# Four value tiles of the softmax branch computed in query rounds 7 to 10 and moved into their place by DMA

## The chip, the cores and the metric

The kernel runs on one core of one Trainium2 chip. The metric is device time in microseconds (us) of one launch; the time before is the median of three runs, 1008.59 us (1005.69 to 1008.81). The profile is one separate execution of the same kernel. PE is TensorE, DVE is VectorE, ACT is ScalarE, POOL is GpSimd, and SP is the engine that issues the DMAs.

## What is computed

Two attention branches over the same x (2048 tokens, 448 features, 16 heads of 28) are mixed by a gate for each token:

```python
x = A_x
g = sigmoid((x * gate_w).sum(-1, keepdims=True))
a = linear_attention(x, A_wqkv, w_phi) @ A_wo      # phi = [softmax(p), softmax(-p)], o = phi_q (phi_k^T v) / (phi_q sum phi_k)
b = softmax_attention(x, B_wqkv) @ B_wo            # softmax(q k^T / sqrt(28)) v
return g * a + (1 - g) * b
```

All is float32; products with x use a high part and a low part of each operand, so that one 128-token tile of a projection is 11 matmuls of 128x448.

## The kernel before, in words

**Front.** x, its parts and the queries and keys of branch B are made first (a scratch array in DRAM, `qkd`, holds the latter). Then one loop (L763) walks over rounds i = 0 to 42. In rounds 0 to 15 it makes the keys' features and the values of branch A and sums them (L483). From i = 16 on the round has a second number, q = i - 16, and this text counts by q, 0 to 26.

**The query rounds.** In rounds q = 0 to 15 PE multiplies x tile q with the folded query weights (`pq`, L801), ACT copies it out (`pcq`, L449), DVE and POOL make the two-sided softmax features of it (L451 to L469, with the exponential on ACT, L460). Three rounds later PE transposes the features (`pft`, L533), and ACT copies them to `fT` (L536). Every second round multiplies the features of 256 tokens with the summed keys and values: `numer(k)`, `pn`, L547, for blocks k = 0 to 7 in round 2k + 5. What follows for a block is a chain over several engines:

- `normalize1` (round 2k + 5): ACT copies the numerators out (`oUa`, L407), and two DMAs gather the denominators (`dena`, L410).
- `normalize2` (end of round 2k + 6): DVE takes the reciprocal (L416, L417), two DMAs write it to DRAM (`rda`, L421), and one DMA reads it back spread over the partitions (`rsa`, L422, 512 KB).
- `normalize3` (round 2k + 9): DVE multiplies (L428).
- `normalize4` (round 2k + 10): ACT rounds it (`oTa`, L436), POOL makes the low part (L437), both in two halves.
- `out_a` (rounds 2k + 11 and 2k + 12): PE multiplies with the output weights (`poa`, 12 matmuls at L117; the third of them is the first to read the low part of the first half), ACT scales by the gate into one of two buffers (`ga`, L599), and a DMA stores that (`gad`, L600).

From round 11 on each round also has one `mx_unit` (`pmb`, `pmd`, L293): scores of branch B whose row maxima are needed later; ACT and DVE reduce them (L296, L298).

**The value tiles of branch B.** In rounds 18 to 25, at the end of the round, `value_b(0)` to `value_b(7)` (L747) make the values of x tiles 0 to 7: 11 matmuls into `pvb`, and one ACT copy into `vb[0]` (L750), the first of two tiles of 8 x 16 x 32 a partition. `vb[0]` is opened in round 18 (L850 to L852), when the features' pool is closed, because it lies in that pool's memory; POOL then sets its columns 28 to 31 (L743, L744). Column 28 is 1.0, so that the product with the values gives the denominator too. After the loop, the value tiles 8 to 15 follow with the last mx units between them (L984 on), and then the softmax attention (L1191 on), whose first read of `vb[0]` is at L1069.

**What sets the order.** The orders of PE, DVE, ACT and POOL are those of the program text: a waiting instruction holds up all behind it on its engine. SP's order is made by a scheduler. All DMAs go through SP's one queue, and the listing of SP's order shows that the DMAs take eight semaphores in turn: a DMA whose semaphore was used eight DMAs before waits until that one has landed, unless it is known already.

PSUM tiles of the front come from four banks in rotation (`ps_s`, L48).

Of the kernel before, what the change touches and what calls it, by code (L numbers as in the profile page):

```python
# [8 lines left out]
F32 = mybir.dt.float32  # L9
# [8 lines left out]
P = 128  # L18
S = 2048
D = 448  # L20
H = 16
DH = 28
GW = 112
NG = 4
NT = S // P
# [15 lines left out]
def gated_mix_kernel(ctx, tc, xT, wqkB, wvB, wvA, wkAT, wqAT, phi, woA, woB,  # L41
# [7 lines left out]
    nc = tc.nc  # L49
# [14 lines left out]
    def ps_s(nm):  # L64
        if turn4:
            turn4.append(nm)
            if len(turn4) % 4 == 0:
                return ps_pv(nm)
        return ps.tile([P, 512], F32, tag="s", name=nm, bufs=psn[0])
# [38 lines left out]
    def weights(place, nm):  # L108
        if place == 1:
            return wp.tile([P, 2, 4, 512], F32R, tag="w1", name=nm)  # L110
        if place == 2:
            return front.tile([P, 2, 4, D], F32R, tag="w2", name=nm)
        return wp.tile([P, 2, 4, 450], F32R, tag="w3", name=nm)
# [13 lines left out]
    def tok_major(dst, t, w, n, mid=None):  # L127

        todo = [(x, w[:, i, b, :n]) for b, x, i in x3(slice(t * P, (t + 1) * P))]
        if mid is None:  # L130
            run(dst[:, :n], todo)
            return
        for i, (l, r) in enumerate(todo):
            mid(i)
            nc.tensor.matmul(dst[:, :n], l, r, start=i == 0, stop=i == len(todo) - 1,  # L135
                             skip_group_check=True)
# [36 lines left out]
    def take_acts():  # L173
        while acts:
            acts.pop(0)()
# [91 lines left out]
    def mx_unit():  # L267

        u = mxs["u"]
        if u == NF:  # L270
            return
        mx_fin()
        take_diffs(2)
        mxs["u"] = u + 1
        gq, r = divmod(u, 16)
        g, qb = divmod(gq, NQ)
        if gq < GM:
            c, qt = divmod(r, 4)
            hp, b = divmod(c, 2)
            col = 64 * gq + 16 * b + 4 * qt + 2 * hp  # L280
            if r in (4, 9):
                pair_query(gq + 1, r // 9)
        else:
            c, qt = divmod(r, QM)
            hp, b = divmod(c, 2)
            col = 64 * gq + 4 * QM * b + 4 * qt + 2 * hp
            if r == 0:
                mx_query(gq)
        qc, kc = mxs[("qp", gq, hp)], mxs[("kp", g, c)]
        pb, pd = ps_mx(f"pmb{u}", False), ps_mx(f"pmd{u}", True)  # L290
        for j in range(4):
            js = slice(32 * j, 32 * j + DH)
            nc.tensor.matmul((pb if j < 2 else pd)[:, j % 2, :], qc[js, qt * P:(qt + 1) * P],  # L293
                             kc[js, :], start=True, stop=True, tile_position=(32 * j, 0))
        rl = rlp.tile([P, 2, 512], F32, tag="rl", name=f"rl{u}", bufs=2 if psn[1] == 3 else 1)
        nc.scalar.activation(rl, pd, AF.Relu)  # L296
        for i in range(2):
            nc.vector.tensor_tensor_reduce(rl[:, i, :], pb[:, i, :], rl[:, i, :], 1.0, LOWEST,  # L298
                                           ALU.add, ALU.max, part[:, col + i:col + i + 1])
        if gq < GM and qt == 3 and qb == NQ - 1:  # L300
            pair_load(g + 1, c)
        if gq == GM and qt == QM - 1:
            mx_load(g, c)
        if r == 15:
            mx_reduce(gq)
# [157 lines left out]
    def features2(f, nm):  # L463

        f2 = f[:, :, :2 * DH].rearrange("p h (s f) -> p h s f", f=DH)
        sm = bd.tile([P, H, 2], F32, tag="fsum", name=f"fsum{nm}", bufs=3)
        nc.vector.tensor_reduce(sm, f2, AX.X, ALU.add)
        nc.vector.reciprocal(sm, sm)
        nc.gpsimd.tensor_mul(f2, f2, sm.unsqueeze(3).to_broadcast([P, H, 2, DH]))  # L469
        return f.rearrange("p h f -> p (h f)")  # L470
# [3 lines left out]
    def take_exps(left=0):  # L474
        while len(exps) > left:
            exps.pop(0)()
# [29 lines left out]
    def kv_copy():  # L506

        kvT = ta.tile([P, 2, 512], F32, tag="rs", name="kvT", bufs=2)[:, 0, :]
        k4 = kvT.rearrange("p (g i f) -> p g i f", i=2, f=64)
        nc.gpsimd.memset(k4[:, :, :, 56:], 0.0)  # L510
        nc.scalar.copy(
            k4[:, :, :, :56],
            pkv[:, :224].rearrange("p (g f) -> p g f", f=56).unsqueeze(2).to_broadcast([P, NG, 2, 56]))
        return kvT
# [72 lines left out]
    def load_split(w, nm):  # L587
        for i in range(2):
            nc.sync.dma_start(f32(w[:, i, :, :D]), w_d[nm][:, i])
# [157 lines left out]
    def value_b(t, mid=None):  # L747
        pv = ps_s(f"pvb{t}")
        tok_major(pv, t, wvB_s, D, mid)
        nc.scalar.copy(vb[t // 8][:, t % 8, :, 0:DH], pv[:, :D].rearrange("p (h d) -> p h d", d=DH))  # L750

    pace = {}

# [9 lines left out]
    for i in range(2 * NT + 11):  # L763
        t, q = i, i - NT
        y = q - 1
        tb = y // 2
        take_acts()
        if t < NT and t % 2 == 0:
            mx_unit()
            passes = (55 if t < NT - 4 else 44) + (4 if t >= 4 else 0)  # L770
            pace["n"] = 4 if t >= 4 else 0
            pace["at"] = [passes // 3, 2 * passes // 3] if t in (4, 6, 8) else [passes // 2]
        if q in (0, 1):
            take_exps()
        if part_low:
            part_low.pop()()
        if q == 0:
            woA_s = weights(3, "woA_s")
            wvB_s = weights(2, "wvB_s")
            load_split(woA_s, "woA")  # L780
            load_split(wvB_s, "wvB")

        if t % 2 == 0 and 0 <= t - 4 < NT:
            kv_add(t - 4)
            kv_add(t - 3)
        if q == 2:
            bk_s.close()
            ta_s = ExitStack()
            ta = ta_s.enter_context(tc.tile_pool(name="ta", bufs=1, reuse_waits="tile"))
            KV = ta.tile([P, 512], F32, name="KV")  # L790
            kvT = kv_copy()
            turn4.append("")
            take_exps()
        if t < NT:
            pk = ps_s(f"pk{t}")
            tok_major(pk, t, wkA_s, D, tick)
            fk[t] = features1(pk, f"k{t}", nc.gpsimd)
            take_exps(1)
        if 0 <= q < NT:
            pq = ps_s(f"pq{q}")  # L800
            tok_major(pq, q, wqA_s, D)  # L801
        if q == 0:
            fk[NT - 1] = features2(fk[NT - 1], f"k{NT - 1}")
        if q in (1, 2):
            fq[q - 1] = features2(fq[q - 1], f"q{q - 1}")
        if 0 <= q < NT:
            fq[q] = features1(pq, f"q{q}", nc.vector if 0 < q < 11 else nc.gpsimd)
        if 0 <= t - 1 < NT - 1:
            fk[t - 1] = features2(fk[t - 1], f"k{t - 1}")
        if q in (0, 1) or q >= 11:  # L810
            mx_unit()
        if y >= 9 and y % 2 and tb - 4 < 8:
            oTs[tb - 4] = normalize4(ta, num.pop(tb - 4), f"a{tb - 4}", 2)
        if y >= 4 and y % 2 == 0 and tb - 2 < 8:
            numer(tb - 2)
        if q > 0:
            take_exps(int(q < NT))
        if q == 3:
            kv_out(kvT)
        if 2 <= q - 1 < NT:  # L820
            fq[q - 1] = features2(fq[q - 1], f"q{q - 1}")
        take_subs()
        if t == 1:
            pair_load(0, 3)
        if y >= 8 and y % 2 == 0 and tb - 4 < 8:
            num[tb - 4] = normalize3(*num[tb - 4], 2)
        if t < NT:
            value_a(t)
            if t % 2 and t < NT - 4:
                proj_qk(NP + t // 2, ev)  # L830
                if t < 8:
                    part_low.append(part_high(t // 2))
        if q in (0, 1):
            proj_qk(NP + 6 + q, ev)
        take_lows()
        if 2 <= i < 6:
            fold(wqA_s, "q", i - 2)
        if q == 1:
            ev_s.close()
        if q == 1:  # L840
            gates()
        if y < 9 or y % 2:
            if y >= 2 and y - 2 < NT:
                turn(y - 2)
        if 0 <= y - 10 < NT:
            out_a(y - 10)
            out_a2(y - 10)
        if y >= 9 and y % 2 == 0 and y - 2 < NT:
            turn(y - 2)
        if q == NT + 2:  # L850
            bd_s.close()
            vb = [value_tile(0)]  # L852
        if 0 <= q - NT - 2 < 8:
            value_b(q - NT - 2)
        if y >= 5 and y % 2 and tb - 2 < 8:
            num[tb - 2] = normalize2(ta, *num[tb - 2], f"a{tb - 2}", 2, True)
    ta_s.close()
# [442 lines left out]
```

## Time and profile before

| | |
|---|---|
| median of 3 runs | 1008.59 us |
| the profiled execution's own time | 1007.98 us |
| its span (first to last instruction) | 1006.2 us |
| PE busy | 997.0 us (99% of the span) |
| ACT, DVE, POOL busy | 80%, 67%, 24% |
| mean granted TensorE clock | 0.998 |
| rounds q = 7 to 10 | 200.2 to 215.0 us |
| rounds q = 18 to 26 | 262.9 to 310.7 us |

How to read a row of a timeline: start in us, duration in us, engine, line and operation, output<-inputs, sizes, how many instructions were merged, and in square brackets the idle time of that engine before the row with what ended it. A row of a table by windows has, for each engine, busy us and in brackets the number of instructions, in the order PE, weight load, DVE, ACT, POOL, and at its end the granted TensorE clock, the busy share of the 16 DMA engines and GB/s.

### The profile page before, as it was taken

The numbers are of one execution on the slowest core, as the hardware profiler recorded it, in microseconds if no ns is written. First come the engines' busy times: TensorE is split into PE (matmuls) and PEld (weight loads), VectorE is DVE, ScalarE is ACT, GpSimd is POOL, SyncE is SP. The second block draws the span as 40 slices with busy tenths as digits, with TensorE's granted clock in tenths as the row PEclk, the third lists the DMA queues.
The fourth block names the chain that finished last, engine by engine and source line by source line (L and its number), as shares of the span: only waits on it lengthen the run. The fifth ranks groups of instructions, "written<-read, shape, count | busy, mean of one in ns | idle before, by whom it ended". The sixth has DMA issues, their size and how long they took to land.

```text
span 1006.2 us, 17986 instructions
## 1 busy us (share of the span) xinstructions
PE 997.0 (99%) x6472; PEld 556.3 (55%) x6472; DVE 679.2 (67%) x1340; ACT 803.4 (80%) x1532; POOL 237.4 (24%) x215
## 2 busy tenths in 40 slices
PE   9999999989999999999999999999999999999998
PEld 8878888868888433333333333333333334455656
DVE  5557766997535688888888888888887874544202
ACT  5445545667743899999999999999999999979682
POOL 1265456687436103111011110101201011001010
PEclk9999999999999999999999999999999999999999
DMA  8976313312235703333532123431324345515131
GB/s 296 313 234 212 118 50 108 113 47 82 92 116 137 158 10 84 83 75 77 120 69 75 44 67 86 102 90 49 90 52 97 81 98 145 147 38 148 60 107 55
DMA packets 67769, 106.23 MB, mean 106 GB/s; under 512 B 18368, under 2 KB 28208, under 8 KB 67680
## 3 DMA queue, kind: packets, MB, share of 16 engines
q1 hardware_dynamic: 67680, 105.08, 38.6%
q8 instruction: 51, 0.84, 0.4%
q14 instruction: 38, 0.31, 0.1%
HBM read 73.21 MB, written 31.45 MB: 104 GB/s over the span
## 4 chain that ended last, share of the span: by engine, by line
PE 77%; DVE 0%; ACT 0%; issue 0%
PE st L965 28%; PE pv L1069 25%; PE pm L330 9%; PE poa L117 4%; PE pob L117 3%; PE pvb L135 2%; PE pvb L117 2%; PE pq L117 1%; PE pmb L293 1%; PE pft L533 1%; PE poL L1107 1%; PE pn L547 1%; PE poL L1177 0%; DVE part L341 0%; PE pr L1162 0%; PE pd L1152 0%
## 5 line engine op out<-in xcount | busy, mean ns | idle before, releaser
L968 ACT ACTIVATE p<-st 128x512 f32<-128x512 f32 x1020 | 529.3, 639 | 25.7 <-PE st L965 25.7
L341 DVE TENSOR_REDUCE part<-pm 128x1 f32<-128x512 f32 x477 | 304.7, 685 | 134.8 <-PE pm L330 134.8
L965 PE MATMUL st<-qst,kst 128*128 128x512 f32 x1020 | 303.1, 423 | 0.4 <-DVE acc L1084 0.4
L1069 PE MATMUL pv<-p,vb 128*32 128x512 f32 x2048 | 266.1, 603 | 0.0
L965 PEld LDWEIGHTS st<-qst,kst 128*128 128x128 f32 x1020 | 167.9, 187 | 99.4 <-ACT p L968 48.9
L334 ACT ACTIVATE rl<-pm 128x512 f32<-128x512 f32 x212 | 132.2, 624 | 15.5 <-PE pm L330 13.4
L330 PEld LDWEIGHTS pm<-kc,qc 28*128 28x128 f32 x848 | 40.5, 181 | 177.8 <-issue 104.8
L428 POOL TENSOR_TENSOR oUb<-oUb,rsb 128x512 f32<-128x512 f32 x15 | 19.4, 1291 | 457.0 <-DMA rsb<-rdb 212.2
L338 DVE CUSTOM_DVE_ANT_0 rl<-pm,rl 128x512 f32<-128x512 f32 x159 | 108.2, 681 | 0.0
L330 PE MATMUL pm<-kc,qc 28*128 28x512 f32 x848 | 107.3, 495 | 0.0
L1069 PEld LDWEIGHTS pv<-p,vb 128*32 128x32 f32 x2048 | 45.4, 108 | 94.1 <-issue 87.4
L298 DVE CUSTOM_DVE_ANT_0 rl<-pmb,rl 128x512 f32<-128x512 f32 x88 | 56.6, 681 | 36.9 <-ACT rl L296 36.9
L117 PE MATMUL pqk<-XH,wB 128*128 128x512 f32 x192 | 59.3, 397 | 0.0
L296 ACT ACTIVATE rl<-pmd 128x1024 f32<-128x1024 f32 x44 | 45.4, 1031 | 8.2 <-PE pmd L293 4.5
L623 ACT CAST ev<-pqk 128x512 fp32r<-128x512 f32 x28 | 16.1, 589 | 38.6 <-PE pqk L117 28.8
L117 PE MATMUL poa<-woA_s,oTa 128*128 128x448 f32 x192 | 44.6, 382 | 0.0
L117 PEld LDWEIGHTS pqk<-XH,wB 128*128 128x128 f32 x192 | 35.4, 188 | 8.5 <-issue 1.5
L1084 DVE SCALAR_TENSOR_TENSOR acc<-pob,gate,acc 128x448 f32<-128x448 f32 x12 | 8.2, 681 | 47.2 <-PE pob L117 47.2
L117 PEld LDWEIGHTS poa<-woA_s,oTa 128*128 128x128 f32 x192 | 35.9, 194 | 6.9 <-issue 4.2
L204 POOL TENSOR_TENSOR kc<-kc,kd 28x512 fp32r<-28x512 f32 x12 | 15.4, 1281 | 101.6 <-DMA kc<-qkd 45.8
L624 DVE TENSOR_TENSOR ev<-pqk,ev 128x512 fp32r<-128x512 f32 x28 | 19.1, 690 | 28.8 <-ACT ev L623 28.7
L135 PE MATMUL pva<-wvA_s,XH 128*128 128x450 f32 x128 | 37.6, 371 | 0.0
(163 smaller groups left out, 1175.8 us busy)
## 6 DMA issues: line engine op xcount, KB each, us to landing
qkd<-ev SPq DMA_DIRECT2D x28, 512.0 KB
qst<-qkd SPq DMA_DIRECT2D x64, 224.0 KB
kst<-qkd SPq DMA_DIRECT2D x64, 224.0 KB
od<-oTb SPq DMA_DIRECT2D x48, 112.0 KB
rsa<-rda SPq DMA_DIRECT2D x8, 512.0 KB
rsb<-rdb SPq DMA_DIRECT2D x15, 256.0 KB
kc<-qkd SPq DMA_DIRECT2D x64, 56.0 KB
gad<-ga SPq DMA_DIRECT2D x16, 224.0 KB
```

Source lines behind the costliest of these rows:

```text
L117: nc.tensor.matmul(dst, l, r, start=i == 0, stop=i == len(todo) - 1)
L135: nc.tensor.matmul(dst[:, :n], l, r, start=i == 0, stop=i == len(todo) - 1, skip_group_check=True)
L296: nc.scalar.activation(rl, pd, AF.Relu)
L298: nc.vector.tensor_tensor_reduce(rl[:, i, :], pb[:, i, :], rl[:, i, :], 1.0, LOWEST, ALU.add, ALU.max, part[:, col + i:col + i + 1])
L330: nc.tensor.matmul(pm[j], mxs[("qc", gq)][js, qt * P:(qt + 1) * P], mxs[("kc", g, kb)][js, :], start=True, stop=True, tile_position=(32 * ...
L334: nc.scalar.activation(rl, pm[kb], AF.Relu if kb < 3 else AF.Copy)
L338: nc.vector.tensor_tensor_reduce(r, pm[j], r, 1.0, LOWEST, ALU.add, ALU.max, part[:, col + j:col + j + 1])
L341: nc.vector.tensor_reduce(part[:, col + j:col + j + 1], pm[j], AX.X, ALU.max)
L428: (nc.gpsimd if n == 1 else nc.vector).tensor_mul(oU, oU, rs)
L965: nc.tensor.matmul(st, kst_of[(gq // NQ, kt // 4)][:, j, (kt % 4) * P:(kt % 4 + 1) * P], qst_of[gq][:, j, :], start=True, stop=True)
L968: nc.scalar.activation(p, st, AF.Exp, scale=SCALE)
L1069: nc.tensor.matmul(pv[32 * j:32 * j + 32, :], vb[kt // 8][:, kt % 8, 4 * g + j, :], pt[j], start=kt == 0, stop=kt == NT - 1, tile_position ...
```

## The change

Four value tiles (0 to 3) are computed behind the query tiles of rounds 7 to 10. They go into two tiles of their own (`ve0`, `ve1`, 4 KB a partition each), made in round 2, whose columns 28 to 31 POOL sets then. When `vb[0]` is opened in round 18, two DMAs of 512 KB copy them into it. The value tiles 4 to 7 follow in rounds 18 to 21, so that rounds 22 to 25 have none. The number of matmuls and of ACT copies is unchanged; four POOL memsets and two DMAs are added.

```diff
     def value_b(t, mid=None):
         pv = ps_s(f"pvb{t}")
         tok_major(pv, t, wvB_s, D, mid)
-        nc.scalar.copy(vb[t // 8][:, t % 8, :, 0:DH], pv[:, :D].rearrange("p (h d) -> p h d", d=DH))
+        v = early[t // 2][:, t % 2] if t < 4 else vb[t // 8][:, t % 8]
+        nc.scalar.copy(v[:, :, 0:DH], pv[:, :D].rearrange("p (h d) -> p h d", d=DH))
...
             kvT = kv_copy()
+            early = [ta.tile([P, 2, 512], F32, tag="rl2", name=f"ve{i}", bufs=2) for i in range(2)]
+            early = [e.rearrange("p t (h d) -> p t h d", d=32) for e in early]
+            for e in early:
+                nc.gpsimd.memset(e[:, :, :, 28:], 0.0)
+                nc.gpsimd.memset(e[:, :, :, 28:29], 1.0)
...
             fk[t - 1] = features2(fk[t - 1], f"k{t - 1}")
+        if 7 <= q < 11:
+            value_b(q - 7)
         if q in (0, 1) or q >= 11:
             mx_unit()
...
         if q == NT + 2:
             bd_s.close()
             vb = [value_tile(0)]
-        if 0 <= q - NT - 2 < 8:
-            value_b(q - NT - 2)
+            for k, e in enumerate(early):
+                nc.sync.dma_start(vb[0][:, 2 * k:2 * k + 2], e)
+        if 0 <= q - NT - 2 < 4:
+            value_b(q - NT + 2)
```

## Prediction

> **What bounds the kernel now.** I read the page first: is there an engine that never rests?
>
> ```profile
> span 1006.2 us, 17986 instructions
> PE 997.0 (99%) x6472; PEld 556.3 (55%) x6472; DVE 679.2 (67%) x1340; ACT 803.4 (80%) x1532; POOL 237.4 (24%) x215
> ```
>
> PE is busy 99% of the span. Work that is moved on PE but not removed can gain only where PE stands still, or where its clock is low. So I next read PE's timeline over the query rounds, and then a table by windows around the one large gap.
>
> ```profile
> 217.38 0.50 PE L293 MATMUL pmd<-kp,qp 28*128 28x512 f32 x2
> 221.00 1.55 PE L547 MATMUL pn<-fT,KV 56*32 56x256 f32 x32 [3.12 <-ACT fT L536]
> 222.47 3.89 PE L117 MATMUL poa<-woA_s,oTa 128*128 128x448 f32 x12
> ...
> 217.80:221.00 3.20, 0.08 (x5) 0.01 (x1) 3.07 (x5) 2.52 (x5) 1.94 (x2) 1.00 0.24 93
> 221.00:226.50 5.50, 5.50 (x47) 3.99 (x48) 5.42 (x11) 3.82 (x7) 5.31 (x5) 0.69 0.15 45
> ...
> 266.00:311.00 45.00, 44.70 (x253) 36.42 (x251) 15.42 (x41) 22.09 (x36) 12.77 (x12) 1.00 0.34 106
> 311.00:330.00 19.00, 18.58 (x94) 15.92 (x95) 11.32 (x14) 6.80 (x11) 14.52 (x10) 1.00 0.83 173
> ```
>
> In round 11 PE stands still for 3.12 us until ACT has copied `fT`. Then the granted clock is 0.69 for 5.5 us, which loses 5.5 x 0.31 = 1.70 us. The gap is worth 3.12 + 1.70 = 4.82 us. From 266 to 330 us PE stands still for 0.30 + 0.42 us in all, so the rest of the front has nothing to gain. Why was `fT` late? The timelines of ACT, DVE and SP:
>
> ```profile
> 218.48 1.14 ACT L436 CAST oTa<-oUa 128x512 fp32r<-128x512 f32 x2 [3.58 <-DVE oUa L428]
> 219.53 0.94 ACT L460 ACTIVATE feat<-feat 128x896 f32<-128x896 f32 x1
> 220.38 1.05 ACT L536 COPY fT<-pft 128x512 f32<-128x512 f32 x2
> ...
> 215.75 2.70 DVE L428 TENSOR_TENSOR oUa<-oUa,rsa 128x1024 f32<-128x1024 f32 x1 [0.23 <-DMA rsa<-rda]
> ...
> 207.89 0.54 SPq L422 DMA_DIRECT2D rsa<-rda  x1
> ```
>
> ACT stood 3.58 us before the first `oTa` for DVE's product with block 0's `rsa`, and `fT` was behind it on ACT. That `rsa`, 512 KB, took 215.75 - 207.89 = 7.86 us to land. So the gap comes from block 0's normalisation chain, not from PE's own work.
>
> **The change part by part.** *Moved tiles.* One value tile and one `out_a` on the chain of waits, and the starts of `pq` in rounds 7, 10 and 11 on PE's timeline:
>
> ```profile
> 300.00 2.27 PE pvb L117 x11
> 308.06 2.65 PE poa L117 x12
> ...
> 200.20 0.65 PE L117 MATMUL pq<-wqA_s,XH 128*128 128x448 f32 x2
> 211.86 0.64 PE L117 MATMUL pq<-wqA_s,XH 128*128 128x448 f32 x2
> 214.96 0.65 PE L117 MATMUL pq<-wqA_s,XH 128*128 128x448 f32 x2
> ```
>
> A tile is 2.27 us of PE, so four are 9.08 us. They are added ahead of round 11 and taken out of rounds 22 to 25. Of the first part the gap should swallow 4.82. With three tiles before it, `pq` of round 10 starts at 211.86 + 6.81 = 218.7, three us after `rsa` has landed, and ACT does its casts, exponential and first `fT` copy (1.14 + 0.85 + 0.5) behind the fourth tile's copy at 218.7 + 2 x 2.27 + 0.5 = 223.7, by 226.2; PE arrives at `pn` only at 217.88 + 9.08 = 227.0. So round 18 starts 9.08 - 4.82 = 4.26 us later than before.
>
> The four ACT copies move with their tiles; ACT has room in rounds 7 to 10, where a round of PE grows from (214.96 - 200.20) / 4 = 3.7 to 6 us.
>
> *Memsets in round 2.* Four of POOL, like this one:
>
> ```profile
> 183.43 0.15 POOL L510 MEMSET kvT<- 128x64 f32 x1
> 186.83 1.71 POOL L469 TENSOR_TENSOR feat<-feat,fsumq 128x896 f32<-128x896 f32 x1 [3.25 <-ACT pcq L449]
> 267.76 0.53 POOL L743 MEMSET vb<- 128x512 f32 x1
> ```
>
> Between 0.15 and 0.53 us each, 0.6 to 2.1 together, in a POOL gap of 3.25 us. I cost them at nothing; without that cover they would cost at most 2.1.
>
> *What the tail gives back.* If PE never waited in rounds 18 to 26, they would end 9.08 earlier relative to their start, and the sum would be -4.82. But blocks 6 and 7 have the same chain, and I now read SP and DVE there. All times that follow are on the scale of before, as if round 18 began at the same moment.
>
> ```profile
> 264.69 0.54 SPq L422 DMA_DIRECT2D rsa<-rda  x1
> 267.02 1.24 SPq L421 DMA_DIRECT2D rda<-dena  x2
> 275.15 0.55 SPq L422 DMA_DIRECT2D rsa<-rda  x1
> 275.80 1.18 SPq L410 DMA_DIRECT2D dena<-oUa  x2
> 284.91 1.14 SPq L421 DMA_DIRECT2D rda<-dena  x2
> 287.87 0.55 SPq L422 DMA_DIRECT2D rsa<-rda  x1
> ...
> 273.61 1.23 DVE L428 TENSOR_TENSOR oUa<-oUa,rsa 128x1024 f32<-128x1024 f32 x1 [1.58 <-DMA rsa<-rda]
> 284.31 0.18 DVE L416 TENSOR_SCALAR dena<-dena 128x32 f32<-128x32 f32 x1 [5.91 <-DMA dena<-oUa]
> 297.58 1.23 DVE L428 TENSOR_TENSOR oUa<-oUa,rsa 128x1024 f32<-128x1024 f32 x1 [3.13 <-DMA rsa<-rda]
> ```
>
> Three `rsa` (blocks 5, 6, 7) follow one another. Block 5's takes 273.61 - 264.69 = 8.92 us, block 7's 297.58 - 287.87 = 9.71. A tiny `dena` issued right behind block 6's lands 8.5 us later, while `rda` with nothing ahead needs 287.87 - 285.48 = 2.39 from its second issue (284.91 + 0.57), 1.8 of it after the issue: small DMAs stand behind an `rsa`. This chain runs at the DMAs' pace, not at PE's. How near is PE to it already?
>
> ```profile
> 298.02 0.64 ACT L599 ACTIVATE ga<-poa,gate 128x448 f32<-128x448 f32 x1 [4.91 <-DMA gad<-ga]
> 298.55 0.52 ACT L750 COPY vb<-pvb 128x448 f32<-128x448 f32 x1
> 298.97 1.04 ACT L296 ACTIVATE rl<-pmd 128x1024 f32<-128x1024 f32 x1
> 299.88 1.15 ACT L436 CAST oTa<-oUa 128x512 fp32r<-128x512 f32 x2
> ...
> 300.59 2.53 POOL L437 TENSOR_TENSOR oTa<-oUa,oTa 128x512 fp32r<-128x512 f32 x2 [8.46 <-ACT oTa L436]
> ...
> 302.63 2.73 PE L117 MATMUL poa<-woA_s,oTa 128*128 128x448 f32 x12
> ```
>
> POOL has the first low half at 300.59 + 1.27 = 301.86; the third matmul of `out_a(14)` at 302.63 + 0.44 = 303.07 needs it. The slack is 1.2 us. Between `numer(7)` and `out_a(14)` stood six value tiles and now stand three: PE arrives 6.81 us earlier, and finds nothing.
>
> *The moves* sit in that chain. In the listing of the changed order SP issues the first `rda` of block 6, a move, a `gad`, the other move, and then the second `rda`. The first move waits for POOL's memsets of `vb[0]` (the first of the two ends at 268.3), and the second `rda` takes the semaphore of block 5's `rsa`, so it leaves only at 273.6; behind it wait block 7's `dena` and block 6's `rsa`. No row shows a 512 KB move from SBUF to SBUF. The nearest are the `rsa`, of the same size, and two stretches, one with full queues (171 to 183 us) and one with the `rsa` alone:
>
> ```profile
> rsa<-rda SPq DMA_DIRECT2D x8, 512.0 KB
> ...
> DMA packets 1665, 4.10 MB, mean 342 GB/s; under 512 B 101, under 2 KB 1125, under 8 KB 1664
> ...
> 287.90:290.00 2.10, 2.10 (x12) 1.93 (x11) 1.21 (x4) 1.53 (x3) 1.65 (x2) 1.00 0.25 84
> ```
>
> At 342 GB/s 1.05 MB take 3.1 us, at 84 GB/s 12.5. An `rsa` keeps a quarter of the DMA engines busy (0.25); the moves, spread over all partitions, are likelier to run at the first rate. The second `rda` then lands between 273.6 + 2.4 = 276.0 (the moves done beside block 5's `rsa`) and 273.6 + 3.1 + 1.8 = 278.5 (moves wholly behind it); I take the middle, 277.2, and 283.7 as the far end at the slow rate (issued about 269.4, + 12.5 + 1.8).
>
> [...]
>
> *The sum for the tail.* `rsa` of block 6 at 277.2, landed at 277.2 + 8.9 = 286.1; the second `rda` of block 7 again has the semaphore of that `rsa`, so it follows, and `rsa` of block 7 leaves 2.4 later, 288.5, and lands at 288.5 + 9.7 = 298.2. From there as before without the value copy: ACT casts 1.85 later (299.88 - 297.58 - 0.45), POOL starts 0.71 after that and needs 1.27 for the first half: 3.83 in all, 302.0. Ten matmuls at 2.65 / 12 = 0.22 end at 304.2. PE has meanwhile stood since about 302.63 - 6.81 = 295.8, first until ACT's half at 300.6, so for 4.8 us, longer than the 3.12 above: the same slow stretch, 1.70 us, makes it 305.9. Round 26 adds 0.43 + 2.65: 309.0, against 308.06 + 2.65 = 310.71 before. The tail gives back 1.7 of 9.08.
>
> **Sum:** +9.08 - 4.82 - 1.7 = **+2.6 us** on the profiled execution's own 1007.98 us, which is 0.6 below the median: **1010.5 us**. The ends of the unknowns: with 276.0 and both `rsa` at 7.86, block 7's lands at 294.1, PE does not go slow, the tail gives back 7.5 and the sum is -3.2; with 278.5 and 9.7 twice, +4.7.
>
> **Rivals.** *The tail has room after all (faster).* If PE's rounds 18 to 26 never wait, the whole 4.82 is won: 1003.2 us. It decides at `out_a(14)`: block 7's `rsa` would have to land by 302.63 - 6.81 + 0.44 - 3.83 = 292.4 instead of 297.58. For it: `dena` of block 7 is no longer behind block 6's `rsa`. Against it: both `rsa`, 7.86 at the fastest, still follow one another. *The moves are slow.* At 84 GB/s the second `rda` lands at 283.7, 6.5 later, +9; halfway to that, +6: 1014. For it: no row shows such a move. *The gap of round 11 stays*, because ACT is late for another reason: the change doesn't do what it says, and the sum is +9.08 - 1.7: 1015.4 us. Against it: ACT's chain above has only the `rsa` as its cause. *PE keeps its clock in the tail*: 1.70 less, +0.9: 1008.9 us.
>
> [...]
>
> **How the numbers follow.** Forecast 0.53, moves slow 0.17, clock kept 0.15, tail has room 0.10, gap stays 0.05. The forecast's ends, -3.2 and +4.7 around +2.6, put about half of it above +3.0 us; 0.3% is about what a measurement of this kernel can tell from no change. Slower: 0.26 + 0.17 + 0.05 = 0.48; within 0.3%: 0.27 + 0.15 = 0.42; faster 0.10. The range, 1006.0 to 1014.5, holds the forecast and its upper end, the kept clock and most of the slow moves; it leaves out the faster rival (0.10), the gap that stays (0.05) and some 0.05 at the edges.
>
> **What the changed profile would show.** Right: no idle row before `pn` in round 11 and a clock of 1.00 behind it; `rsa` of blocks 6 and 7 landing at about the same distance from round 18 as before; idle rows on PE before `poa` in rounds 23 to 25, some 5 to 7 us in all, released by `oTa`, and a low clock behind them. Wrong: a tail without idle rows, or with PE waiting on something other than `oTa`; an `rsa` of block 7 that lands over 3 us earlier or later than block 5's landing plus 24.6; a PE wait in rounds 2 to 10.

## The result and the profile after

The changed kernel takes 1014.38 us (median of six executions, 1012.92 to 1077.67), the kernel before 1008.70 us beside it (1005.49 to 1009.76). The ratio is 1.0066, 95% interval 1.0049 to 1.0083. The execution of 1077.67 us ran at a mean clock of 0.849 and is left out of the ratio. The profiled execution took 1015.12 us, 7.1 more than that of before, with a mean granted clock of 0.995.

The page of the changed kernel: span, busy times, and the shares of the chain of waits.

```profile
span 1013.3 us, 17995 instructions
PE 1000.8 (99%) x6472; PEld 559.0 (55%) x6472; DVE 677.8 (67%) x1340; ACT 802.5 (79%) x1532; POOL 238.7 (24%) x219
```

PE has the same 6472 matmuls, and yet 3.8 us more busy time: matmuls have become slower somewhere. The two parts of the front tell where. First, PE's timeline of the changed kernel in round 11 and from `out_a(12)` on:

```profile
227.03 1.09 PE L547 MATMUL pn<-fT,KV 56*32 56x256 f32 x32
228.06 2.72 PE L117 MATMUL poa<-woA_s,oTa 128*128 128x448 f32 x12
...
296.87 0.53 PE L293 MATMUL pmb<-kp,qp 28*128 28x512 f32 x2 [3.16 <-ACT rl L296]
298.21 0.79 PE L293 MATMUL pmd<-kp,qp 28*128 28x512 f32 x2 [0.81 <-DVE part L298]
298.93 4.85 PE L117 MATMUL poa<-woA_s,oTa 128*128 128x448 f32 x12
...
308.52 0.49 PE L293 MATMUL pmb<-kp,qp 28*128 28x512 f32 x2 [1.52 <-ACT rl L296]
309.87 0.50 PE L293 MATMUL pmd<-kp,qp 28*128 28x512 f32 x2 [0.85 <-DVE part L298]
310.30 4.26 PE L117 MATMUL poa<-woA_s,oTa 128*128 128x448 f32 x12
```

The gap before `pn` in round 11 is gone. In its place stand four gaps in the last rounds, 3.16 + 0.81 + 1.52 + 0.85 = 6.34 us, and two `out_a` of 4.85 and 4.26 us in the place of 2.72. The same as a table by windows: round 11 and what follows it; the tail, from the start of `out_a(7)` (round 18) to the `qst` memset on DVE that follows the last `out_a`; seven microseconds from the middle of the first slow `out_a` on.

```profile
219.00:231.00 12.00, 12.00 (x95) 10.18 (x94) 9.20 (x18) 9.30 (x17) 9.29 (x7) 1.00 0.16 49
268.59:318.14 49.55, 42.70 (x219) 33.31 (x217) 17.66 (x45) 21.53 (x35) 13.43 (x12) 0.90 0.42 118
300.00:307.00 7.00, 7.00 (x27) 5.29 (x25) 1.96 (x5) 0.20 (x2) 1.13 (x1) 0.71 0.39 112
```

And the same tail in the kernel before, from its `out_a(7)` to the same memset:

```profile
264.16:311.19 47.03, 46.54 (x263) 38.13 (x261) 16.82 (x44) 24.12 (x39) 13.50 (x12) 1.00 0.33 103
```

So the tail starts 268.59 - 264.16 = 4.43 us later and lasts 49.55 - 47.03 = 2.52 longer: 6.95 together, the whole difference. Four tiles, 9.08 us, have left the tail; dense it would be 47.03 - 9.08 = 37.95. It is 11.6 longer than that. I call this the **excess** of the tail (its measured length less its dense length). Of it 49.55 - 42.70 - 0.49 = 6.4 is standing still (0.49 is what before has too), and 42.70 - (46.54 - 9.08) = 5.2 is matmuls at a low clock.

SP's timeline of the changed kernel, with the DMAs of the chain and the two moves (L862), and DVE's products that wait for the `rsa`:

```profile
269.19 0.53 SPq L422 DMA_DIRECT2D rsa<-rda  x1
271.44 0.56 SPq L421 DMA_DIRECT2D rda<-dena  x1
273.13 0.54 SPq L862 DMA_DIRECT2D vb<-ve  x1
274.36 0.75 SPq L862 DMA_DIRECT2D vb<-ve  x1
280.91 0.58 SPq L421 DMA_DIRECT2D rda<-dena  x1
285.34 0.53 SPq L422 DMA_DIRECT2D rsa<-rda  x1
297.19 0.55 SPq L422 DMA_DIRECT2D rsa<-rda  x1
```

```profile
280.92 1.23 DVE L428 TENSOR_TENSOR oUa<-oUa,rsa 128x1024 f32<-128x1024 f32 x1 [4.46 <-DMA rsa<-rda]
294.36 1.23 DVE L428 TENSOR_TENSOR oUa<-oUa,rsa 128x1024 f32<-128x1024 f32 x1 [6.19 <-DMA rsa<-rda]
306.35 1.23 DVE L428 TENSOR_TENSOR oUa<-oUa,rsa 128x1024 f32<-128x1024 f32 x1 [4.88 <-DMA rsa<-rda]
```

The `rsa` of block 5 takes 280.92 - 269.19 = 11.73 us (8.92 before), and that of block 6 leaves 285.34 - 280.92 = 4.42 after it has landed (275.15 - 273.61 = 1.54 before). The chain of waits of the changed kernel has the same two pieces one after the other, and then a `gad` that was issued behind the `rsa` of block 6 and landed with it; what the DMA engines did meanwhile is in the table by windows behind it.

```profile
269.19 11.70 DMA rsa<-rda
...
280.91 4.36 DMA rda<-dena
...
285.92 8.83 DMA gad<-ga
```

```profile
275.00:277.00 2.00, 2.00 (x13) 1.86 (x11) 1.31 (x4) 1.18 (x3) 0.00 (x0) 1.00 1.01 181
277.00:279.00 2.00, 2.00 (x12) 1.82 (x11) 0.00 (x0) 0.00 (x0) 0.00 (x0) 1.00 1.08 250
279.00:281.00 2.00, 2.00 (x12) 1.37 (x11) 0.08 (x1) 0.00 (x0) 0.00 (x0) 1.00 0.49 116
```

With the moves under way all DMA engines are busy (1.01 and 1.08), and yet they move 181 and 250 GB/s.

### The profile page after: what moved, and what is told of

The parts are those of the page before. It is cut to its first block, busy times and chain, and to the rows that moved or that the text cites. A ratio compares the mean times of both kernels' runs of the same rounds, so it can differ in the third digit from the quotient of the medians.

```text
span 1013.3 us, 17995 instructions
## 1 busy us (share of the span) xinstructions
PE 1000.8 (99%) x6472; PEld 559.0 (55%) x6472; DVE 677.8 (67%) x1340; ACT 802.5 (79%) x1532; POOL 238.7 (24%) x219
## 4 chain that ended last, share of the span: by engine, by line
PE 95%; DMA 3%; DVE 1%; ACT 0%; issue 0%; SPq 0%; POOL 0%; ACTq 0%; POOLq 0%
PE st L975 28%; PE pv L1079 25%; PE pm L330 9%; PE pqk L117 6%; PE pk L135 4%; PE pva L135 4%; PE pq L117 4%; PE pob L117 3%; PE poa L117 2%; PE pvb L135 2%; DMA gad<-ga 2%; PE pmb L293 2%; PE pft L533 1%; DMA rsa<-rda 1%; PE pqk L686 1%; PE pvb L117 1%
## 5 line engine op out<-in xcount | busy, mean ns | idle before, releaser
L117 PE MATMUL poa<-woA_s,oTa 128*128 128x448 f32 x192 | 47.1, 398 | 0.0
```

The lines of the kernel that those rows point to most:

```text
L117: nc.tensor.matmul(dst, l, r, start=i == 0, stop=i == len(todo) - 1)
```

## The experiments

Ratios are to the kernel before, five rounds on the same chip, with their 95% intervals; e1 to e4 ran on one chip, e5 to e10 on another. Five experiments (e1 to e4 and e8) are about the moves, e7 is about ACT's buffers, e5 and e6 are about `rsa`, and e9 and e10 about what the others left open. The excess of each tail is read from one table, which stands behind e8.

**e1: no moves.** The value tile's first half is never filled, and the readers take tiles 4 to 7 in the place of 0 to 3.

```diff
-            for k, e in enumerate(early):
-                nc.sync.dma_start(vb[0][:, 2 * k:2 * k + 2], e)
```

> The change without its two moves; the softmax branch reads value tiles 4 to 7 in the place of 0 to 3, so that part of its output is not the reference's. Theory A (the tail goes at the pace of the DMA chain of blocks 5 to 7, and the moves hold that chain up by about 3.7 us): block 5's rsa lands about 9 us after its issue instead of 11.7, block 7's about 3.7 earlier counted from round 18, and the whole is some 4 us shorter than the change, about 2.7 us or 0.27% over before. Theory B (the moves are harmless, the missing value tiles alone make the tail wait): as the change, 0.66% over before.

Measured: 1.0028 (1.0015 to 1.0042). The `rsa` of block 5 takes 277.32 - 268.29 = 9.03 us, where it took 11.73 beside the moves; that of block 6 leaves 279.00 - 277.32 = 1.68 us after it has landed, and the excess falls from 11.6 to 45.05 - 37.95 = 7.1. The moves cost about 4 us, and without them the change is still slower than before. DVE's rows of this run for blocks 5 and 7, SP's issue for block 6, and the tail:

```profile
277.32 1.23 DVE L428 TENSOR_TENSOR oUa<-oUa,rsa 128x1024 f32<-128x1024 f32 x1 [1.74 <-DMA rsa<-rda]
...
300.67 1.23 DVE L428 TENSOR_TENSOR oUa<-oUa,rsa 128x1024 f32<-128x1024 f32 x1 [4.66 <-DMA rsa<-rda]
```

```profile
279.00 0.55 SPq L422 DMA_DIRECT2D rsa<-rda  x1
```

```profile
267.71:312.76 45.05, 40.46 (x219) 31.77 (x217) 16.88 (x44) 22.00 (x35) 13.44 (x12) 0.92 0.36 106
```

This tail starts 3.55 us later than that of before, and the `rsa` of block 7 lands 300.67 - 297.58 = 3.09 later: at nearly the same distance from round 18. Four tiles less on PE did not make it come sooner. That is the pace of the DMA chain.

**e2: the moves late.** POOL sets the columns of the first four tiles only in round 25, so that the moves have to wait for it; they are issued at 309.27, when the last `rsa` has landed.

```diff
-        nc.gpsimd.memset(v[:, :, :, 28:32], 0.0)
-        nc.gpsimd.memset(v[:, :, :, 28:29], 1.0)
+        w = v[:, len(early) * 2 * (1 - i):]
+        nc.gpsimd.memset(w[:, :, :, 28:32], 0.0)
+        nc.gpsimd.memset(w[:, :, :, 28:29], 1.0)
...
+        if q == NT + 9:
+            nc.gpsimd.memset(vb[0][:, :2 * len(early), :, 28:32], 0.0)
+            for k, e in enumerate(early):
+                nc.sync.dma_start(vb[0][:, 2 * k:2 * k + 2], e)
```

> The change with the two moves held back, by the place of a POOL memset that they must follow, until round 25, behind block 7's rsa. Theory A: as without moves, about 0.27% over before (0.15 to 0.45). Theory B: 0.66% over before.

Measured: 1.0035 (1.0022 to 1.0048), not to be told from e1. (Its profiled execution, 1012.95 us, was the longest of twelve, 1009.17 to 1012.95, so its excess in the table is a high one.) The bytes are moved all the same: it is their place in the chain that costs.

**e3: the moves alone.** The kernel before, with its value tiles where they were; the two tiles of their own are filled by a memset, and the two moves are issued in round 18.

```diff
+            for e in early:
+                nc.gpsimd.memset(e, 1.0)
...
+            for k, e in enumerate(early):
+                nc.sync.dma_start(vb[0][:, 2 * k:2 * k + 2], e)
-        if 0 <= q - NT - 2 < 8:
-            value_b(q - NT - 2)
+        if 0 <= q - NT - 2 < 8:
+            value_b((q - NT + 2) % 8)
```

> The kernel before with the two moves alone, at their place in round 18, out of two tiles filled by memset; value tiles 4 to 7 are made in rounds 18 to 21 and 0 to 3 in rounds 22 to 25, over what was moved, so no work leaves the tail. Theory A: block 7's rsa lands about 3.7 us later counted from round 18, PE has 1.2 us of slack at out_a(14), so 2.5 us longer than before and up to 1.7 more by the clock: 0.25 to 0.42% over before. Theory B: no difference.

Measured: 1.0015 (1.0000 to 1.0031), less than the 0.25 to 0.42% expected, and hardly clear of no change. In the trace the moves do hold up the chain: the `rsa` of block 7 lands 298.12 - 262.44 = 35.68 us after the start of `out_a(7)`, 2.3 later than before, and the tail is 1.5 longer (48.49 against 47.03); the rest fell into the slack, for which the prediction had read 1.2. In the profiled execution round 11 has a shorter gap, 1.40 us, which hides part of the cost in its total; why it is shorter is told below, where the prediction's head is weighed.

```profile
220.31 1.15 PE L547 MATMUL pn<-fT,KV 56*32 56x256 f32 x32 [1.40 <-ACT fT L536]
```

**e4: two early tiles** and one move, six value tiles in rounds 18 to 23.

```diff
-        v = early[t // 2][:, t % 2] if t < 4 else vb[t // 8][:, t % 8]
+        v = early[t // 2][:, t % 2] if t < 2 else vb[t // 8][:, t % 8]
...
-        if 7 <= q < 11:
-            value_b(q - 7)
+        if 9 <= q < 11:
+            value_b(q - 9)
...
-        if 0 <= q - NT - 2 < 4:
-            value_b(q - NT + 2)
+        if 0 <= q - NT - 2 < 6:
+            value_b(q - NT)
```

> Only value tiles 0 and 1 go ahead, behind the query tiles of rounds 9 and 10, with one move. Both theories: the gap of round 11 closes (3.12 us against 4.54 of work). Theory A: one move holds the chain by about half, 1.9 us, and one tile less stands before out_a(14), 2.27: with 1.2 of slack PE waits 3.0 there; from -1.8 us without to 0 with a slow clock against before. Theory B: the wait is 2.27 - 1.2 = 1.1 us, so -3.7 us against before.

**e8: two early tiles, the move held back** as in e2.

> Value tiles 0 and 1 in rounds 9 and 10, and their one move held back to round 25. Theory A: gap closed (-4.82), 4.54 us of tiles ahead, tail 4.54 - 1.1 shorter: -3.7 us against before, 0.37% faster, or -2 with a slow stretch in the tail. Theory B gives the same here.

Measured: e4 0.9993 (0.9982 to 1.0005), e8 0.9968 (0.9957 to 0.9978). Two tiles are 4.54 us, about the worth of the gap in round 11, and the tail can give them back where no move stands in its way: e8's is as dense as PE's own work, 42.65 against 47.03 - 4.54 = 42.49. One move in round 18 makes it 46.23, 3.6 more.

The tails of e4, e8, and of e5 and e10 below, one row of each run:

```profile
263.69:309.92 46.23, 44.03 (x241) 35.36 (x239) 16.70 (x44) 23.16 (x37) 13.48 (x12) 0.96 0.38 115
```

```profile
263.73:306.38 42.65, 42.15 (x241) 34.16 (x239) 16.70 (x44) 23.09 (x37) 13.48 (x13) 1.00 0.39 124
```

```profile
267.65:305.62 37.97, 37.48 (x219) 29.87 (x217) 17.07 (x43) 22.01 (x35) 13.54 (x12) 1.00 0.46 147
```

```profile
268.20:313.30 45.10, 41.31 (x219) 32.15 (x216) 16.85 (x44) 21.76 (x35) 13.43 (x12) 0.92 0.42 130
```

| | start of `out_a(7)`, later than before | tail | dense | excess |
|---|---|---|---|---|
| after | 4.43 | 49.55 | 37.95 | 11.6 |
| e1, no moves | 3.55 | 45.05 | 37.95 | 7.1 |
| e2, moves late | 4.57 | 47.05 | 37.95 | 9.1 |
| e7, three `ga` | 3.91 | 48.25 | 37.95 | 10.3 |
| e10, `rda` ahead | 4.0 | 45.10 | 37.95 | 7.2 |
| e5, four `rsa` DMAs | 3.49 | 37.97 | 37.95 | 0.0 |
| e4, two tiles | -0.47 | 46.23 | 42.49 | 3.7 |
| e8, two tiles, move late | -0.43 | 42.65 | 42.49 | 0.2 |
| e3, moves alone | -1.72 | 48.49 | 47.03 | 1.5 |
| e6, before with four `rsa` DMAs | -3.82 | 47.04 | 47.03 | 0.0 |
| e9, two tiles, move late, four `rsa` DMAs | -0.71 | 42.55 | 42.49 | 0.1 |

Each row is one profiled execution. In e2, as in e1, nothing is moved before the last `rsa` has landed, and yet their excesses differ by 2.0; so I read nothing from differences of that size in this table alone.

**e7: a third `ga` buffer.** In the changed kernel PE stands for `rl`, and ACT is at that time at `ga`, whose buffer is free only when its store has landed, and that is the `gad` of the chain above, behind an `rsa`. ACT's timeline and the view of waits of the changed kernel (us in total, times, longest):

```profile
294.83 0.64 ACT L599 ACTIVATE ga<-poa,gate 128x448 f32<-128x448 f32 x1 [8.00 <-DMA gad<-ga]
```

```profile
ACT ga L599 <- DMA gad<-ga: 20.1, 3, 8.0
DVE oUa L428 <- DMA rsa<-rda: 15.5, 3, 6.2
PE pmb L293 <- ACT rl L296: 4.7, 2, 3.2
```

Is this buffer the bound? The run has `bufs=3` in the place of 2 for `ga`.

> The change with three ga buffers instead of two. In the changed profile ACT waits 8.0 and 6.8 us in rounds 21 and 23 for a ga store that stands behind an rsa, and PE's mx unit waits for ACT. Theory C (that hold of ACT is what makes PE wait in the tail): the two waits go and with them most of 6.3 us of idle PE and the slow clock, so 0 to +0.2% over before. Theory A: the ga store and the rsa land together, PE then waits for oTa instead; 0 to 2 us better than the change, +0.45 to +0.66% over before.

Measured: 1.0059 (1.0042 to 1.0075), against 1.0066. ACT's wait for `gad` is gone from the view of waits of this run, and PE waits for DVE instead:

```profile
DVE oUa L428 <- DMA rsa<-rda: 15.0, 3, 5.9
...
PE pmd L293 <- DVE part L298: 5.0, 2, 3.1
```

DVE's `part` stands behind the product that waits for `rsa`. Whichever engine PE meets first, the same DMA is at the end of it. The buffer isn't the bound.

**e5 and e6: `rsa` as four DMAs** of 32 partitions each, with the change (e5) and without it (e6).

```diff
-        nc.sync.dma_start(rs.rearrange("p n q -> p (n q)"),
-                          rd.unsqueeze(1).to_broadcast([4, 32, n * 512]))
+        for j in range(4):
+            nc.sync.dma_start(rs[32 * j:32 * j + 32].rearrange("p n q -> p (n q)"),
+                              rd[j:j + 1].to_broadcast([32, n * 512]))
```

> The change with each rsa of the front issued as four DMAs of 32 partitions in place of one of 128. If the length of the rsa sets the pace of the chain (theory A) and four smaller ones use more of the DMA engines, an rsa lands in about 3 to 5 us, the tail waits little, and the sum is near the prediction's faster rival: -4.8 us against before (-5.5 to -2). If the chain is held by something else (the semaphores' turn, ACT behind the two ga buffers), it stays at +0.4 to +0.66%.

> The kernel before with the same four rsa DMAs. Theory A: block 0's rsa lands some 4 us earlier, DVE's product no longer holds ACT in round 11, the gap and its slow clock (4.82 us) go without moving any value tile: -4.8 us (-5.5 to -3). If the gap has another cause: no difference.

Measured: e5 **0.9955** (0.9940 to 0.9969), 1002.80 us; e6 0.9974 (0.9964 to 0.9984). The tail of e5 has no excess, with both moves in the same place of the program text. (SP's order differs a little: it issues both at 272.20, ahead of both `rda` of block 6, and not between them.) SP's issue of block 7's `rsa`, DVE's product with it, and two microseconds between them by windows:

```profile
288.58 1.77 SPq L427 DMA_DIRECT2D rsa<-rda  x4
```

```profile
295.62 1.22 DVE L433 TENSOR_TENSOR oUa<-oUa,rsa 128x1024 f32<-128x1024 f32 x1
```

```profile
290.60:292.60 2.00, 2.00 (x11) 1.68 (x9) 1.31 (x4) 1.69 (x3) 0.76 (x1) 1.00 0.69 193
```

The product has no idle time before it, and begins 7.0 us after the issue. The DMAs are busy at 0.69 with 193 GB/s, where one `rsa` had 0.25 with 84 in the kernel before.

In e6, without the moved tiles, the gap of round 11 shrinks to 1.27 us but stays, where the expectation had it go. With a faster chain the moved tiles fill it, and the tail can give back all 9.08 us: the change itself is then worth 0.9974 - 0.9955 = 0.19%. The intervals of the two ratios overlap, but the executions do not: e5 took 1002.60 to 1003.27 us and e6 1004.29 to 1005.33, side by side.

```profile
218.57 1.15 PE L552 MATMUL pn<-fT,KV 56*32 56x256 f32 x32 [1.27 <-ACT fT L541]
```

**e9: two early tiles, their move held back to round 25 as in e8, with four `rsa` DMAs.** (The expectation says round 17; the edit is that of e8.)

> Two early tiles, the move held back to round 17 behind POOL's late memset, and rsa of 512 KB as four DMAs of 32 partitions each. The run with four early tiles and four DMAs has a tail as dense as PE's own work, 37.97 us against 47.03 - 9.08 = 37.95, and 0.9955 of the time before; the run with two early tiles and the move held back has 42.65 and 0.9968. Theory P (with the normalisation chain faster, nothing but PE's own work is left in this front): the place of the tiles no longer matters, the two tiles less in the head are two more in the tail, and the ratio is 0.995 to 0.997, not to be told from four early tiles. Rival M (moves still cost something, hidden in the other run): one move less saves 1 to 2 us, ratio 0.9935 to 0.9945.

Measured: 0.9962 (0.9947 to 0.9976), 1003.02 us, with a dense tail of 42.55. Theory P holds: neither the number of early tiles nor their moves tell any more in the time.

**e10: `rda` ahead of the moves.** What is the price of a move made of, the time for which `rda` of block 6 is held, or the bandwidth that is taken from `rsa`? The instruction of the moves stands in round 26 of the program text, eight rounds later than in the changed kernel (the expectation says earlier). SP's order is made by a scheduler, and still has the moves beside the `rsa` of blocks 5 and 6, but behind both `rda` of block 6.

```diff
+        if q == NT + 10:
             for k, e in enumerate(early):
                 nc.sync.dma_start(vb[0][:, 2 * k:2 * k + 2], e)
```

> The change with one difference: the instruction of the moves stands eight rounds earlier in the program text, so that SP's order becomes: both halves of rda of block 6, the first move, a gad, rsa of block 6, the second move, dena of block 7. With the changed kernel, rsa of block 6 left 4.42 us after rsa of block 5 had landed, where it is 1.68 in the run without moves. Theory Q (the queue and the semaphore's turn: rda of block 6 is held behind the moves, bytes matter little): the moves are still issued while rsa of block 5 is on its way, rsa of block 6 leaves again about 1.7 us after it, the excess of the tail falls from 11.6 to 8 to 9 us, ratio 1.0030 to 1.0040. Theory W (the moves take the DMA engines from whatever rsa they run beside, 216 GB/s for 1.05 MB, about 4.8 us): rsa of block 5 or 6 is stretched by 2 to 3 us wherever the moves run, rsa of block 7 lands again over 36.5 us after the start of out_a(7), and the ratio is 1.0055 to 1.0070. If it lies between, both have a part, and the landing of rsa of block 7 tells how much of each.

Measured: 1.0052 (1.0034 to 1.0070), seven executions between 1009.88 and 1013.69: between the two forecasts, 1.0030 to 1.0040 and 1.0055 to 1.0070. The profiled one, 1010.50 us, looks like theory Q: SP issues the `rsa` of block 6 280.15 - 278.62 = 1.53 us after that of block 5 has landed, between the moves, the excess is 7.2, and the `rsa` of block 7 lands 303.18 - 268.20 = 34.98 us after the start of `out_a(7)`, where theory W had over 36.5. SP's timeline of this run, and DVE's row for block 7:

```profile
271.04 1.14 SPq L421 DMA_DIRECT2D rda<-dena  x2
272.72 1.97 SPq L863 DMA_DIRECT2D vb<-ve  x1
...
280.15 0.56 SPq L422 DMA_DIRECT2D rsa<-rda  x1
280.77 0.53 SPq L863 DMA_DIRECT2D vb<-ve  x1
```

```profile
303.18 1.23 DVE L428 TENSOR_TENSOR oUa<-oUa,rsa 128x1024 f32<-128x1024 f32 x1 [1.26 <-DMA rsa<-rda]
```

But four of the seven took 1012.0 to 1013.7 us, and of these there is no trace. In times this kernel can't be told from the changed one. How the price of the moves divides between the queue and the bandwidth stays open.

## Why the prediction was right and wrong

The forecast was 1010.5 us and the time 1014.38. By its time this is the rival called "the moves are slow" (1014), which had 0.17. That the number fits is in part luck: the rival took a point halfway to the rate of 84 GB/s, without a row for it, and counted one slow stretch where there are two.

- **The head: right in time, and its cause read too narrowly.** Forecast +4.26, measured +4.43. The idle row before `pn` is gone, and the clock is 1.00 behind it. But the `rsa`, to which the prediction put the gap of 3.12 us, held DVE's product of block 0 for only 0.23 us. That let POOL's `feat` begin 0.09 us ahead of the product, which then took 2.70 us. In e3 and e6 the product began (216.54 and 214.86) before the reciprocal that `feat` waits for had ended (216.21 + 0.35 = 216.56 and 214.59 + 0.35 = 214.94). There it took 1.22 and 1.16, and the gap was 1.40 and 1.27; behind it the clock was 1.00 in e3 (221 to 231 us), and in e6 `out_a` took 2.85 us, where it took 3.89 in the kernel before. So about 1.3 us of the gap has nothing to do with the `rsa`: in e6 the product has no idle time before it, and PE still stands 1.27 us for `fT`. DVE's row of e3:

```profile
216.54 1.22 DVE L428 TENSOR_TENSOR oUa<-oUa,rsa 128x1024 f32<-128x1024 f32 x1
```

- **Memsets and copies at nothing: right.** POOL has its four instructions more, and the head has 0.17 us beyond its sum.
- **The tail finds nothing for PE: right, and shown by e1, e5 and e8.** The `rsa` of blocks 5 to 7 set its pace: without moves it is still 7.1 over dense, with four DMAs for each `rsa` it is 0. The rival "the tail has room" fell for four tiles; for two it holds, as e8 shows.
- **The price of the moves: the step that failed.** The second `rda` of block 6 was put at 277.2 on the scale of before, the middle of 276.0 and 278.5. It landed at 285.3 - 4.4 = 280.9. That it takes the semaphore of block 5's `rsa` was read rightly: on the changed kernel's own scale it left at 280.91, as that landed (280.92). Two terms were too small. The `rsa` of block 5, taken to land at 273.6 as before, came at 280.92 - 4.43 = 276.5, with the moves beside it and the DMA engines at 1.01 and 1.08; and `rda` then took 4.36 us in the place of 2.4. Six profiled executions agree on this. With both moves in round 18 block 5's `rsa` takes 11.73 us (the change), 11.01 (e7) and 10.13 (e3), and that of block 6 leaves 4.42, 4.44 and 4.28 us after it has landed; without moves there (before, e1, e2) it is 8.92, 9.03 and 8.83, and 1.54, 1.68 and 1.42. The rate of 342 GB/s came from a stretch with full queues; this one had full engines at 181 and 250 GB/s, `rsa` included. Of the two ends, 276.0 and 278.5, the later was the nearer. The far end, 283.7, was nearer than the middle. From there it goes on unchanged: the `rsa` of block 7 landed at 306.35 - 4.43 = 301.9, forecast 298.2. That is 3.7 of the 4.2 us by which the tail missed (-1.7 forecast, +2.5 measured).
- **One slow stretch: too few.** There are two, behind the gaps of block 6 and of block 7, and they cost 5.2 us in the place of 1.70. The forecast of an excess of 9.08 - 1.7 = 7.4 agrees with e1's 7.1, which has no moves, though the forecast had counted them: this error and that in the price of the moves partly stood for one another.
- **What releases PE: wrong in name.** The gaps (6.34 us, forecast 5 to 7) end with `rl` and `part`, not with `oTa`. An mx unit ahead of `out_a` meets ACT or DVE while they wait. e7 shows that the name doesn't matter.
- **"PE keeps its clock": fell.** The mean clock of the tail is 0.90. Its 0.15 was an estimate, and no row of before spoke for it.
- **The test by block 5's landing plus 24.6 was badly chosen.** It gave 306.35 - 280.92 = 25.4, as if all were well, since block 5's own `rsa` was late.

## What to carry to other kernels

Work taken out of a stage is a gain only if the stage's slowest chain gets shorter with it: compare, before the move, the distance between the landings of the transfers that pace the stage with the work that is to be left in it. A copy that "only" makes room is placed by what is behind it in the DMA queue, and by what runs beside it: here the `rsa` of block 5 took 11.73 us with the moves and 9.03 without them (e1), and that of block 6 left 4.42 and 1.68 us after it had landed. Here the gain lay in the transfer that paced the tail, and once that was faster the same change was worth something.

## What the runs showed of the hardware that was not expected

- One 512 KB read from 4 rows to 128 partitions kept 0.25 of the DMA engines busy (287.90 to 290.00) and took 7.9 to 9.7 us in the kernel before; as four DMAs of 32 partitions it had 0.69 (e5, 290.60 to 292.60), and the kernel was 0.26% faster by that alone (e6).
- Two copies of 512 KB from SBUF to SBUF, with an `rsa` beside them, kept all engines busy (1.01 and 1.08) at only 181 and 250 GB/s in the changed kernel, from 275 to 279 us.
- Behind idle stretches of 1.9 to 3.2 us on PE the matmuls ran at a lower clock: behind 3.12 us in the kernel before the clock was 0.69 for 5.5 us; behind 3.16 us in the changed kernel, and behind 2.49 us in e10, an `out_a` took 4.85 us in the place of 2.72, and behind 1.92 us in e7 one took 4.27. Behind 1.40 us in e3 the clock was 1.00. Whether the same gap costs the clock in one execution and not in another, no run here shows.
- The kernel before has two groups of times. In 28 of 69 executions of it that ran beside the experiments the mean clock was 1.000, and they took 1004.8 to 1006.8 us, median 1005.4; in the other 41 it was 0.997 to 0.999, and they took 1006.5 to 1010.5, median 1008.5. The profiled one is of the second group, and of the first there is no trace. I take the race of DVE and POOL at block 0's product (next point) to part them, as e3's trace has the short gap and keeps its clock; that isn't shown. All executions of e6 lie at 1004.3 to 1005.3, near the first group, so most of what e6 gains is that the second doesn't occur. If so, a good part of the 4.82 us at which the prediction priced the gap was there to be had only in some of the executions.
- Where DVE's product of block 0 and a `feat` product on POOL ran at the same time, the one that began later took longer than where it began first. In the kernel before DVE's product (215.75, 2.70 us) began just behind POOL's `feat` (1.71 us); in the changed kernel DVE began first, took 1.16 us, and POOL's same `feat` took 2.49. The lengths are near what they would be if the later one stood until the other had ended: 1.16 plus POOL's remaining 215.66 + 1.71 - 215.75 = 1.62 is 2.78, where 2.70 was measured, and POOL's 1.71 plus DVE's remaining 221.48 + 1.16 - 221.71 = 0.93 is 2.64, where 2.49 was measured. That it stood, and for what, no run here shows. POOL's row of before, and DVE's and POOL's of the changed kernel:

```profile
215.66 1.71 POOL L469 TENSOR_TENSOR feat<-feat,fsumq 128x896 f32<-128x896 f32 x1 [0.73 <-DVE fsumq L468]
```

```profile
221.48 1.16 DVE L428 TENSOR_TENSOR oUa<-oUa,rsa 128x1024 f32<-128x1024 f32 x1
```

```profile
221.71 2.49 POOL L469 TENSOR_TENSOR feat<-feat,fsumq 128x896 f32<-128x896 f32 x1 [3.09 <-DVE fsumq L468]
```
